# Attention, gated layer and leaky layer on one core: where the last 20 weight blocks of layer 2 are converted

## The chip, the cores and the metric

The kernel runs on one core of a Trainium2 chip. The metric is the device time of one execution, in microseconds (us); of several runs the median counts. TensorE (PE; PEld is its weight load) multiplies, VectorE (DVE), ScalarE (ACT) and GpSimd (POOL) work on tiles, SyncE (SP) issues the DMA transfers. Every engine takes its instructions in the order of the program.

## The reference

Three layers in a row, in float32. An attention whose keys and queries are hashed into buckets (2 batches, 8 heads, 768 positions, 64 columns), then a gated layer (1536 tokens, 512 to 1536 to 512), then a layer with a leaky activation (512 to 2048 to 512). What matters here are the two layers behind the attention:

```python
g = x @ w_gate                                  # layer 1
silu = g * (1.0 / (1.0 + np.exp(-g)))
x = silu * (x @ w_val) @ w_out
h = x @ w_in                                    # layer 2
g = np.maximum(h, 0.0) + alpha * np.minimum(h, 0.0)
out = g @ w_out
```

The weights reach the chip as 64-bit numbers (two 32-bit words each) and have to be converted to float32 there.

## The kernel before

The 1536 tokens are three chunks of 512 (`W`). Layer 1 runs in three stages, `stage1(0)`, `stage1(1)` and `stage1(2)`; the first two are interleaved with the attention, the third runs alone. Layer 2 runs in three passes, `stage2(1)`, `stage2(2)`, `stage2(0)`. "The third stage" is `stage1(2)`, "pass 1" is `stage2(1)`; pass 1 reads chunk 1, which the second stage of layer 1 left, and not what the third stage computes.

**Weights as two parts.** TensorE gets a float32 weight as a high part (rounded on ScalarE, L580, "h") and a low part (the rest, L587, "l": alternately on GpSimd and VectorE), and an activation likewise (`xh`, `xl`; `gh` by L635 on ScalarE, `gl` by L638 on GpSimd). A block of 128 x 512 weights costs 12 matmuls, three (`mm3`, L643 to L645, or `mm_out`, L648 to L650) for each of four slices. The low part is read by the third matmul of a slice in `mm3` and by the second in `mm_out`.

**The third stage.** It loops over f = 0 to 11 (`F1`). Each f multiplies two blocks of 12 matmuls (gate, value); ScalarE, VectorE and GpSimd then form `gh` and `gl` (L620, L623, L626, L635, L638). After f = 4 and f = 8 and at the end, `quad` multiplies four output blocks of 12 matmuls. So it has 24 + 12 blocks. Their high and low parts were stored in DRAM in the first stage; SyncE loads them back (L535, `wb<-w`, 512 KB each) into four buffers. A load waits until TensorE is through with the block four places earlier.

**Layer 2 and its blocks.** A pass loops over f = 0 to 18. At f < 16 it multiplies block hp of f (12 matmuls, into `hp`) and VectorE makes the activation (L629 `leak`, L632 `leak_sum`), ScalarE `gh`, GpSimd `gl`. At f >= 3 (`D2`) it multiplies block op of f - 3 (12 matmuls into `op`). TensorE's order is hp0, hp1, hp2, hp3, op0, hp4, op1, hp5, op2 and so on. All 32 blocks of layer 2 stay in one tile `w` (`fin.w`) as float32. The first 12 in order of use ("early") are converted during the first two stages, written to DRAM (`whole`) and read back (L531). The other 20 ("late", op4 to op15 and hp8 to hp15) are converted straight into the tile.

**Converting a block.** SyncE loads the raw block (L523, 512 KB) into one of two buffers (`RAWB`). Then `round64` runs one operation on ScalarE (L540, the low word), two on VectorE (L541, L543, the high word) and one on GpSimd (L545, the sum). `w_late` is a generator: each step converts the block loaded two steps before and loads the next, so 22 steps do 20 blocks. The next raw load into a buffer waits for L540, L541 and L543 of the block that was there.

The scheduler of the language orders the instructions of an engine; those handed to `pin` (raw loads, L540, L541, L545, loads of early blocks) keep the order of the program among themselves.

Of the kernel before, what the change touches and what calls it, by code (L numbers as in the profile page):

```python
# [22 lines left out]
RAWB = 2  # L23
# [25 lines left out]
def lsh_attention_moe_kernel(  # L49
# [23 lines left out]
    F1 = DFF // P  # L73
# [392 lines left out]
    def quad_at(f):  # L466

        return f // QF - 1 if f % QF == 0 and f else None
# [23 lines left out]
    late = [w for w in o2 if w not in early]  # L492
# [22 lines left out]
    def raw_load(w):  # L515
        t = wp.tile([P, 512, 2], I32, tag="raw64", name="raw64", bufs=RAWB)
        if F1O <= w < F2I:
            q, e = divmod(w - F1O, KD)
            src = wblk[F1O + q * QF:F1O + (q + 1) * QF, :, e * P:(e + 1) * P].bitcast(I32)
            pin(nc.sync.dma_start(out=t.rearrange("p (f c) t -> p f (c t)", f=QF),  # L520
                                  in_=src.rearrange("f p c -> p f c")))
        else:
            pin(nc.sync.dma_start(out=t, in_=wblk[w].bitcast(I32).rearrange("p (f t) -> p f t", t=2)))  # L523
        return t
# [12 lines left out]
    def round64(t, a):  # L537

        r = wp.tile([P, 512], I32, tag="wr", name="wr", bufs=2)
        pin(nc.scalar.activation(out=r, in_=t.bitcast(U32)[:, :, 0], func=AF.Copy, scale=float(2.0 ** -29)))  # L540
        pin(nc.vector.tensor_scalar(out=a, in0=t[:, :, 1], scalar1=3, scalar2=0x3FFFFFF8,  # L541
                                    op0=ALU.logical_shift_left, op1=ALU.bitwise_and))
        nc.vector.scalar_tensor_tensor(out=a, in0=t[:, :, 1], scalar=-0x40000000, in1=a,  # L543
                                       op0=ALU.bitwise_and, op1=ALU.bitwise_or)
        pin(nc.gpsimd.tensor_tensor(out=a, in0=a, in1=r, op=ALU.add))  # L545
# [10 lines left out]
    def w_late():  # L556

        rs = []
        for w in late + [None] * RAWB:
            if len(rs) == RAWB or w is None:  # L560
                r, v = rs.pop(0)
                round64(r, fin.w[:, v - F2I, :].bitcast(I32))
            if w is not None:
                rs.append((raw_load(w), w))
            yield
# [45 lines left out]
    def w_next():  # L611
        i = ws.used
        w_ahead(i)
        ws.used += 1
        t = ready.pop(i)
        return [t[:, k, :].rearrange("p (k e) -> p k e", e=P) for k in range(2)]


    def gate_tanh(gp, ex):
        nc.scalar.activation(out=ex, in_=gp, func=AF.Tanh, scale=0.5)  # L620

    def gate_mul(gp, ex):
        nc.vector.scalar_tensor_tensor(out=ex, in0=ex, scalar=1.0, in1=gp, op0=ALU.add, op1=ALU.mult)  # L623

    def gate_val(vp, ex):
        nc.vector.scalar_tensor_tensor(out=ex, in0=ex, scalar=0.5, in1=vp, op0=ALU.mult, op1=ALU.mult)  # L626

    def leak(hp, f, ex):
        nc.vector.tensor_scalar(out=ex, in0=hp, scalar1=0.0, scalar2=al[:, f:f + 1], op0=ALU.min, op1=ALU.mult)  # L629

    def leak_sum(hp, ex):
        nc.vector.scalar_tensor_tensor(out=ex, in0=hp, scalar=0.0, in1=ex, op0=ALU.max, op1=ALU.add)  # L632

    def split_h(h, ex):
        nc.scalar.activation(out=h, in_=ex, func=AF.Copy)  # L635

    def split_l(h, l, ex):
        nc.gpsimd.tensor_tensor(out=l, in0=ex, in1=f32(h), op=ALU.subtract)  # L638

    def mm3(pt, w, ah, al_, first, last):  # L640

        h, l = w
        nc.tensor.matmul(pt, lhsT=h, rhs=ah, start=first, stop=False)  # L643
        nc.tensor.matmul(pt, lhsT=h, rhs=al_, start=False, stop=False)  # L644
        nc.tensor.matmul(pt, lhsT=l, rhs=ah, start=False, stop=last)  # L645
# [16 lines left out]
    def gate_bank():  # L662
        tag = at.tag["gates"][at.gates % len(at.tag["gates"])]
        at.gates += 1
        return at.ps.tile([P, W], F32, tag=tag, name="gp", bufs=at.nb[tag])

    def quad(q, acc, gs, xh, xl):

        for e in range(KD):
            h, l = flat(w_next())  # L670
            yp = gate_bank()
            for i in range(QF):
                sl = slice(i * P, (i + 1) * P)
                mm3(yp, (h[:, sl], l[:, sl]), *gs[q * QF + i], i == 0, i == QF - 1)
                if i == 1:
                    yield
            if q == 0:
                nc.scalar.activation(out=acc[:, e, :], in_=yp, func=AF.Copy)
            else:
                nc.vector.tensor_tensor(out=acc[:, e, :], in0=yp, in1=acc[:, e, :], op=ALU.add)  # L680
            if q == F1 // QF - 1:
                nc.scalar.activation(out=xh[:, e, :], in_=acc[:, e, :], func=AF.Copy)
                eng = nc.gpsimd if ws.busy else nc.vector
                eng.tensor_tensor(out=xl[:, e, :], in0=acc[:, e, :], in1=f32(xh)[:, e, :], op=ALU.subtract)
            yield

    def stage1(c, conv=()):

        xh, xl = chunk(c)
        acc = at.lt.tile([P, KD, W], F32, tag="acc", name="acc", bufs=1)  # L690
        gs = {}
        conv = iter(conv)
        for f in range(F1):
            for _ in range(-(-(len(late) + RAWB) // F1)):
                next(conv, 0)
            ps = []
            ex = tmp()
            for tag in "GY":
                pt = gate_bank()
                w = w_next()  # L700
                for kk in range(KD):
                    mm3(pt, (w[0][:, kk, :], w[1][:, kk, :]), xh[:, kk, :], xl[:, kk, :], kk == 0, kk == KD - 1)
                    if kk == 1:
                        yield
                if tag == "G":
                    gate_tanh(pt, ex)
                    gate_mul(pt, ex)
                    yield
            gs[f] = g_tiles()
            gate_val(pt, ex)  # L710
            split_h(gs[f][0], ex)
            split_l(gs[f][0], gs[f][1], ex)
            yield
            q = quad_at(f)
            if q is not None:
                yield from quad(q, acc, gs, xh, xl)
        yield from quad(F1 // QF - 1, acc, gs, xh, xl)

    def stage2(c):

        xh, xl = chunk(c)
        t0 = c * W
        ops, gs = [], {}
        for f in range(F2 + D2):
            if f < F2:
                tag = ("G", "Y", "G", "po")[f % 4]
                hp = at.ps.tile([P, W], F32, tag=tag, name="hp2", bufs=at.nb[tag])
                w = w_next()
                for kk in range(KD):
                    mm3(hp, (w[0][:, kk, :], w[1][:, kk, :]), xh[:, kk, :], xl[:, kk, :], kk == 0, kk == KD - 1)  # L730
                ex = tmp()
                gs[f] = g_tiles()
                leak(hp, f, ex)
                leak_sum(hp, ex)
                split_h(gs[f][0], ex)
                split_l(gs[f][0], gs[f][1], ex)
            if f >= D2:
                fo = f - D2
                h, l = flat(w_next())
                a, b_ = gs.pop(fo)  # L740
                if fo == 0:
                    ops = [at.ps.tile([P, 512], F32, tag=t, name="op", bufs=at.nb[t]) for t in "SSST"]
                for i in range(W // P):
                    sl = slice(i * P, (i + 1) * P)
                    mm_out(ops[i], a[:, sl], b_[:, sl], h, l, fo == 0, fo == F2 - 1)
        for i in range(W // P):
            out_rows(t0 + i * P, ops[i], i, fin.pool.tile([P, W], F32, tag="ob", name="ob", bufs=4))
# [4 lines left out]
    def tmp():  # L752
        if fin.pool:
            return fin.pool.tile([P, W], F32, tag="ex2", name="ex2", bufs=NEX[1])
        return at.lt.tile([P, W], F32, tag="ex", name="ex", bufs=NEX[0])

    def g_tiles():
        return [at.lt.tile([P, W], F32R, tag=t, name=t, bufs=NG1) for t in ("gh", "gl")]
# [10 lines left out]
    def chunk(c):  # L769

        if c not in CH:
            CH[c] = [tx.tile([P, KD, W], F32R, tag=n, name=n, bufs=2) for n in ("xh", "xl")]
        return CH[c]
# [74 lines left out]
    ws.busy = False  # L848
    at.gates = 0
    at.tag = dict(gates="GYTS")  # L850
    for _ in stage1(2, w_late()):
        pass
    for n, c in enumerate((1, 2, 0)):
        if n == 1:
            CH.pop(0)
            for i, t in enumerate(chunk(0)):
                nc.sync.dma_start(out=f32(t).rearrange("p k w -> p (k w)"), in_=spill[i])
        stage2(c)


# [50 lines left out]
```

## Time and profile before

| what | value |
|---|---|
| median of three runs | 864.99 us (863.51 to 867.81) |
| profiled execution, its own time | 866.91 us |
| its span, first to last instruction | 865.1 us |
| TensorE busy / mean granted clock | 827.0 us / 0.988 |
| VectorE, ScalarE, GpSimd busy | 524.5, 449.4, 366.7 us |
| third stage, first to last matmul start | 493.2 to 599.3 us |
| pass 1 of layer 2 begins | 599.3 us |

The rows in this document come from one profiled execution. Times are microseconds from the start of its span; the profiled execution's own time also holds what lies around the span. A row's "idle before" is the time in which its engine had nothing to run, with the operation that ended it. The granted clock is the share of TensorE's full clock; it has two levels, 1.2 and 2.4 GHz, and a number between them is a mean over the stretch.

### The profile page before, as it was taken

The page shows a single profiled execution, that of the slowest core. Times are in us where ns is not written, and L with a number is a line of the kernel's source. Part 1 is how long each engine was busy: PE and PEld are TensorE (multiplying, and loading weights), DVE is VectorE, ACT ScalarE, POOL GpSimd, SP SyncE. Part 2 cuts the span into 40 slices and gives each one's busy share as a digit, 9 for nine tenths or more (in the row PEclk, how much of TensorE's full clock was granted, in tenths as well). Part 3 has the DMA queues.
Part 4 walks back from the last instruction along what each step waited for, and adds up shares of the span by engine and source line. Part 5 has one row for each costly group of instructions (what it writes and reads, how often), then busy time and mean ns, then how long its engine had stood idle before and what let it go on. Part 6 is the DMA issues. An engine that isn't in the chain of part 4 may idle for free.

```text
span 865.1 us, 11230 instructions
## 1 busy us (share of the span) xinstructions
PE 827.0 (96%) x4022; PEld 692.2 (80%) x4022; DVE 524.5 (61%) x789; ACT 449.4 (52%) x738; POOL 366.7 (42%) x304
## 2 busy tenths in 40 slices
PE   6899899999898999999999999999999999999997
PEld 4788688877787888888888777777888888888886
DVE  6878988888887765765675373755433343334332
ACT  7887787677766655555543232314333333333331
POOL 5212437575553532323221453634544354435441
PEclk9999999999999999999999999999999999999999
DMA  9120446776655437454535777876000300010001
GB/s 238 39 73 28 168 144 219 247 255 222 202 197 183 159 117 283 159 196 170 180 128 192 237 268 279 322 273 214 1 1 0 147 1 1 0 49 1 1 0 49
DMA packets 57287, 122.03 MB, mean 141 GB/s; under 512 B 16912, under 2 KB 29200, under 8 KB 56720
## 3 DMA queue, kind: packets, MB, share of 16 engines
q1 hardware_dynamic: 56080, 118.51, 40.2%
q0 software_dynamic: 1008, 2.75, 1.4%
q8 instruction: 32, 0.52, 0.2%
q14 instruction: 23, 0.19, 0.1%
q10 hardware_dynamic: 144, 0.05, 0.0%
HBM read 94.03 MB, written 27.26 MB: 140 GB/s over the span
## 4 chain that ended last, share of the span: by engine, by line
PE 70%; DVE 11%; ACT 7%; DMA 5%; issue 3%; POOL 2%; SPq 0%; DVEq 0%; ACTq 0%; POOLq 0%
PE po L335 9%; PE gp L645 8%; PE gp L644 8%; PE gp L643 8%; PE op L649 5%; PE hp L644 5%; PE op L650 5%; PE hp L645 5%; PE op L648 5%; PE hp L643 5%; DMA raw<-in_wblk_dram 4%; PE S L286 2%; PE S L285 2%; DVE se L322 2%; ACT se L287 2%
## 5 line engine op out<-in xcount | busy, mean ns | idle before, releaser
L638 POOL TENSOR_TENSOR gl<-ex,gh 128x512 fp32r<-128x512 f32 x84 | 111.0, 1322 | 186.2 <-ACT gh L635 185.9
L335 PE MATMUL po<-se,vv 128*128 128x256 f32 x576 | 140.6, 384 | 2.9 <-ACT se L327 2.7
L643 PE MATMUL gp<-xh,wb 128*128 128x512 f32 x288 | 122.3, 425 | 3.2 <-DMA wb<-w 3.2
L335 PEld LDWEIGHTS po<-se,vv 128*128 128x128 f32 x576 | 107.8, 191 | 20.8 <-ACT se L327 5.2
L629 DVE TENSOR_SCALAR ex<-hp,al 128x512 f32<-128x512 f32 x48 | 36.1, 751 | 136.3 <-PE hp L645 136.3
L645 PE MATMUL gp<-xh,wb 128*128 128x512 f32 x288 | 113.7, 395 | 0.0
L644 PE MATMUL gp<-xl,wb 128*128 128x512 f32 x288 | 113.4, 394 | 0.2 <-POOL xl L364 0.2
L635 ACT ACTIVATE gh<-ex 128x512 fp32r<-128x512 f32 x84 | 52.9, 630 | 109.4 <-DVE ex L632 67.6
L580 ACT ACTIVATE wb<-w 128x512 fp32r<-128x512 f32 x96 | 60.5, 632 | 92.6 <-PE hp L645 78.3
L545 POOL TENSOR_TENSOR wt<-wt,wr 128x512 int32<-128x512 int32 x48 | 63.5, 1325 | 93.3 <-DVE wt L543 45.3
L327 ACT ACTIVATE se<-se 128x1536 f32<-128x1536 f32 x48 | 71.3, 1485 | 53.6 <-DVE se L322 53.5
L287 ACT ACTIVATE se<-S 128x512 f32<-128x512 f32 x144 | 80.6, 592 | 26.6 <-PE S L286 24.0
L285 PE MATMUL S<-QA,kt 128*128 128x256 f32 x288 | 82.5, 312 | 7.7 <-ACT se L287 3.0
L322 DVE SCALAR_TENSOR_TENSOR se<-se,mb 128x1536 f32<-128x1536 f32 x48 | 83.7, 1743 | 1.8 <-PE mb L317 1.7
L286 PE MATMUL S<-qb,kt 76*128 76x256 f32 x288 | 75.4, 290 | 4.7 <-ACT qb L204 4.5
L643 PE MATMUL hp<-xh,wb 128*128 128x512 f32 x192 | 74.7, 389 | 0.0
L644 PE MATMUL hp<-xl,wb 128*128 128x512 f32 x192 | 74.7, 389 | 0.0
L645 PE MATMUL hp<-xh,wb 128*128 128x512 f32 x192 | 74.7, 389 | 0.0
L648 PE MATMUL op<-wb,gh 128*128 128x512 f32 x192 | 74.7, 389 | 0.0
L649 PE MATMUL op<-wb,gh 128*128 128x512 f32 x192 | 74.7, 389 | 0.0
L650 PE MATMUL op<-wb,gl 128*128 128x512 f32 x192 | 74.7, 389 | 0.0
L587 POOL TENSOR_TENSOR wb<-w,wb 128x512 fp32r<-128x512 f32 x48 | 62.4, 1301 | 23.6 <-ACT wb L580 23.5
(98 smaller groups left out, 1677.3 us busy)
## 6 DMA issues: line engine op xcount, KB each, us to landing
wb<-w SPq DMA_DIRECT2D x72, 512.0 KB, 4.0
raw<-in_wblk_dram SPq DMA_DIRECT2D x68, 512.0 KB, 4.1
w<-wb SPq DMA_DIRECT2D x36, 512.0 KB, 2.9
qr<-in_q_dram SPq DMA_DIRECT2D x24, 256.0 KB, 3.2
nat<-in_k_dram SPq DMA_DIRECT2D x8, 384.0 KB, 3.4
vv<-in_v_dram SPq DMA_DIRECT2D x16, 192.0 KB, 5.0
whole<-wt SPq DMA_DIRECT2D x12, 256.0 KB, 2.2
w<-whole SPq DMA_DIRECT2D x12, 256.0 KB, 6.1
```

Of the source, the lines that this page charges most:

```text
L285: nc.tensor.matmul(pt[:, i, :], lhsT=ka[:, sl], rhs=qa, start=True, stop=False)
L286: nc.tensor.matmul(pt[:, i, :], lhsT=kb[:, sl], rhs=qb, start=False, stop=True)
L287: nc.scalar.activation(out=u.se[:, 2 * j:2 * j + 2, :], in_=pt, func=AF.Copy)
L322: nc.vector.scalar_tensor_tensor(out=u.se, in0=u.se, scalar=FLOOR, in1=u.mx[:, None, :].to_broadcast([P, NC, GQ]), op0=ALU.max, op1=ALU.su ...
L335: nc.tensor.matmul(it.po[:, u.x, :], lhsT=VV[it.b, it.p][:, kb, u.x * D:u.x * D + P], rhs=u.se[:, kb, :], start=kb == 0, stop=kb == NC - 1)
L638: nc.gpsimd.tensor_tensor(out=l, in0=ex, in1=f32(h), op=ALU.subtract)
L643: nc.tensor.matmul(pt, lhsT=h, rhs=ah, start=first, stop=False)
L644: nc.tensor.matmul(pt, lhsT=h, rhs=al_, start=False, stop=False)
L645: nc.tensor.matmul(pt, lhsT=l, rhs=ah, start=False, stop=last)
L648: nc.tensor.matmul(pt, lhsT=gh, rhs=h, start=first, stop=False)
L649: nc.tensor.matmul(pt, lhsT=gh, rhs=l, start=False, stop=False)
L650: nc.tensor.matmul(pt, lhsT=gl, rhs=h, start=False, stop=last)
```

## The change

Before, the third stage takes two steps of `w_late` at each f (22 steps over 12 f, rounded up), and all are done at f = 10. After, one step is taken ahead of the stage, one at each of its 12 f, and the other nine one at each f of pass 1, f = 0 to 8.

```diff
-    def stage1(c, conv=()):
+    def stage1(c, conv=iter(())):
...
-        conv = iter(conv)
         for f in range(F1):
-            for _ in range(-(-(len(late) + RAWB) // F1)):
-                next(conv, 0)
+            next(conv, 0)
...
-    def stage2(c):
+    def stage2(c, conv):
...
         for f in range(F2 + D2):
+            next(conv, 0)
             if f < F2:
...
-    for _ in stage1(2, w_late()):
+    late_steps = w_late()
+    for _ in range(RAWB - 1):
+        next(late_steps, 0)
+    for _ in stage1(2, late_steps):
         pass
...
-        stage2(c)
+        stage2(c, late_steps)
```

On SyncE, in the third stage (f = 0 to 3), where `wb<-w` are the stored blocks of layer 1 and `raw` the late blocks:

```order
 L523 DMA raw_4787<-in_wblk_dram 128x1024
-L523 DMA raw_4794<-in_wblk_dram 128x1024
 L535 DMA wb<-w_78 128x1024
 L535 DMA wb<-w_79 128x1024
-L523 DMA raw_4839<-in_wblk_dram 128x1024
-L523 DMA raw_4846<-in_wblk_dram 128x1024
+L523 DMA raw_4832<-in_wblk_dram 128x1024
 L535 DMA wb<-w_80 128x1024
-L523 DMA raw_4891<-in_wblk_dram 128x1024
-L523 DMA raw_4898<-in_wblk_dram 128x1024
 L535 DMA wb<-w_81 128x1024
+L523 DMA raw_4877<-in_wblk_dram 128x1024
```

Pairs of raw loads between the weight loads have become single ones, one for two weight loads.

On GpSimd, from the last gl of the third stage into pass 1, before. The weights' low halves (L587) are in turn those of hp0, hp2, op0, op1, op2, op3; the gl (L638) behind them are those of f = 0 to 4:

```order
-L638 TENSOR_TENSOR gl<-ex_5426,gh 128x512
-L587 TENSOR_TENSOR wb_5517<-w_4738,wb_5517 128x512
-L587 TENSOR_TENSOR wb_5541<-w_4738,wb_5541 128x512
-L587 TENSOR_TENSOR wb_5570<-w_4738,wb_5570 128x512
-L587 TENSOR_TENSOR wb_5618<-w_4738,wb_5618 128x512
-L638 TENSOR_TENSOR gl<-ex_5561,gh 128x512
-L638 TENSOR_TENSOR gl<-ex_5585,gh 128x512
-L587 TENSOR_TENSOR wb_5662<-w_4738,wb_5662 128x512
-L638 TENSOR_TENSOR gl<-ex_5609,gh 128x512
-L638 TENSOR_TENSOR gl<-ex_5633,gh 128x512
-L587 TENSOR_TENSOR wb_5701<-w_4738,wb_5701 128x512
-L638 TENSOR_TENSOR gl<-ex_5677,gh 128x512
```

The same place after the change, from the low halves of hp0 and hp2 on; the low halves are now wb_5525 for op0, wb_5587 for op1 and, two rows behind the last one shown, wb_5638 for op2:

```order
+L587 TENSOR_TENSOR wb_5458<-w_4738,wb_5458 128x512
+L587 TENSOR_TENSOR wb_5489<-w_4738,wb_5489 128x512
+L545 TENSOR_TENSOR w_4738<-w_4738,wr 128x512
+L638 TENSOR_TENSOR gl<-ex_5509,gh 128x512
+L545 TENSOR_TENSOR w_4738<-w_4738,wr 128x512
+L638 TENSOR_TENSOR gl<-ex_5540,gh 128x512
+L587 TENSOR_TENSOR wb_5525<-w_4738,wb_5525 128x512
+L545 TENSOR_TENSOR w_4738<-w_4738,wr 128x512
+L587 TENSOR_TENSOR wb_5587<-w_4738,wb_5587 128x512
+L638 TENSOR_TENSOR gl<-ex_5571,gh 128x512
+L545 TENSOR_TENSOR w_4738<-w_4738,wr 128x512
+L638 TENSOR_TENSOR gl<-ex_5602,gh 128x512
```

The low half of op0 stood ahead of every gl of the pass and now stands behind two conversions and two gl; then a conversion, gl of f = 3 and another conversion stand ahead of the low half of op2.

## Rows read from the trace of the kernel before

**Rows 1.** The page, section 1: busy us (share of the span) and instructions by engine.

```profile
PE 827.0 (96%) x4022; PEld 692.2 (80%) x4022; DVE 524.5 (61%) x789; ACT 449.4 (52%) x738; POOL 366.7 (42%) x304
```

**Rows 2.** Timeline of PE, third stage: start us, us, instruction, [idle before <-releaser].

```profile
493.19 0.39 PE L643 MATMUL gp<-xh,wb 128*128 128x512 f32 x1
...
517.44 0.39 PE L645 MATMUL gp<-xh,wb 128*128 128x512 f32 x1
520.99 0.76 PE L643 MATMUL gp<-xh,wb 128*128 128x512 f32 x1 [3.16 <-DMA wb<-w]
...
524.05 0.40 PE L644 MATMUL gp<-xl,wb 128*128 128x512 f32 x1
...
560.90 0.39 PE L645 MATMUL gp<-gh,wb 128*128 128x512 f32 x1
562.05 0.50 PE L643 MATMUL gp<-gh,wb 128*128 128x512 f32 x1 [0.77 <-DMA wb<-w]
562.39 0.40 PE L644 MATMUL gp<-gl,wb 128*128 128x512 f32 x1
...
599.33 0.39 PE L643 MATMUL hp<-xh,wb 128*128 128x512 f32 x1
```

**Rows 3.** Windows: PE, PEld, DVE, ACT, POOL busy, PEclk, DMA share, GB/s.

```profile
517.40:525.30 7.90, 4.74 (x15) 3.51 (x15) 3.93 (x6) 2.33 (x4) 4.00 (x4) 0.78 0.95 354
```

**Rows 4.** Waits of SyncE's queue, 493.2 to 599.3: us, times, longest.

```profile
SPq L523 <- DVE w L543: 30.9, 16, 3.0
```

**Rows 5.** Timeline of SyncE around the long hole.

```profile
514.11 2.35 SPq L523 DMA_DIRECT2D raw<-in_wblk_dram  x2
516.51 0.90 SPq L535 DMA_DIRECT2D wb<-w  x2
```

**Rows 6.** Timeline of DVE, conversions of the third stage.

```profile
505.03 0.42 DVE L541 TENSOR_SCALAR w<-raw 128x512 int32<-128x512 int32 x1
505.49 0.69 DVE L543 SCALAR_TENSOR_TENSOR w<-raw,w 128x512 int32<-128x512 int32 x1
...
511.77 1.54 DVE L541 TENSOR_SCALAR w<-raw 128x512 int32<-128x512 int32 x1 [0.78 <-DMA raw<-in_wblk_dram]
...
514.41 1.66 DVE L543 SCALAR_TENSOR_TENSOR w<-raw,w 128x512 int32<-128x512 int32 x1
```

**Rows 7.** Timeline of POOL beside them.

```profile
511.73 1.29 POOL L638 TENSOR_TENSOR gl<-ex,gh 128x512 fp32r<-128x512 f32 x1 [0.70 <-ACT gh L635]
514.18 1.34 POOL L545 TENSOR_TENSOR w<-w,wr 128x512 int32<-128x512 int32 x1 [1.16 <-DVE w L543]
```

**Rows 8.** Groups by line, 493.2 to 599.3: busy us, mean ns, idle before.

```profile
L545 POOL TENSOR_TENSOR w<-w,wr 128x512 int32<-128x512 int32 x20 | 26.5, 1327 | 30.2 <-DVE w L543 20.4 <-ACT wr L540 9.9
L543 DVE SCALAR_TENSOR_TENSOR w<-raw,w 128x512 int32<-128x512 int32 x20 | 20.3, 1014 | 0.7
...
L541 DVE TENSOR_SCALAR w<-raw 128x512 int32<-128x512 int32 x20 | 15.4, 770 | 6.8 <-DMA raw<-in_wblk_dram 6.6
```

**Rows 9.** Windows, a stretch of pass 1; columns as in rows 3.

```profile
619.30:660.00 40.70, 40.70 (x181) 33.73 (x180) 14.21 (x22) 13.86 (x22) 19.62 (x16) 1.00 0.00 0
```

**Rows 10.** DMA issues, 480 to 606: count, size, median us to landing.

```profile
wb<-w SPq DMA_DIRECT2D x38, 512.0 KB, 4.5
...
w<-whole SPq DMA_DIRECT2D x12, 256.0 KB, 6.1
```

**Rows 11.** Timeline of POOL in pass 1.

```profile
640.37 1.29 POOL L638 TENSOR_TENSOR gl<-ex,gh 128x512 fp32r<-128x512 f32 x1 [2.90 <-ACT gh L635]
641.62 1.28 POOL L587 TENSOR_TENSOR wb<-w,wb 128x512 fp32r<-128x512 f32 x1
```

**Rows 12.** Timeline of PE, two holes in the attention.

```profile
237.94 0.39 PE L286 MATMUL S<-qb,kt 76*128 76x256 f32 x1 [2.21 <-ACT qb L204]
...
264.05 0.39 PE L286 MATMUL S<-qb,kt 76*128 76x256 f32 x1 [2.29 <-ACT qb L204]
```

**Rows 13.** Windows around these holes; columns as in rows 3.

```profile
262.00:269.00 7.00, 4.95 (x22) 4.39 (x23) 3.45 (x6) 5.35 (x10) 2.24 (x2) 0.76 0.50 184
236.00:243.00 7.00, 5.06 (x30) 4.48 (x31) 4.50 (x8) 5.63 (x11) 4.11 (x4) 1.00 0.66 231
```

## The prediction

> **What bounds the kernel now.** I read the page first, then TensorE row by row in the third stage, then the queue that ends its holes, then the engines behind that queue. The page gives TensorE 96% of the span [rows 1]: only its holes and its slow clock can be won or lost. In the third stage of layer 1 its matmuls follow each other every 0.2267 us (107 steps from 493.19 to 517.44 [rows 2]). The stage has 432 of them (24 gate and 12 output blocks of 12), 97.9 us at that pace; it takes 599.33 - 493.19 = 106.1 us, 8.2 more [rows 2]:
> - 517.44 to 520.99: a hole for a weight block, 3.55 - 0.23 = 3.32 us. The seven steps behind it take 3.06 us in place of 1.59, at a granted clock of 0.78 over the stretch (part of it at the lower level, 1.2 GHz) [rows 3]: 1.47.
> - Three short holes for weight blocks, each with the slow step behind it. The largest is shown: from 560.90 to 562.39 two steps take 1.49 us in place of 0.45, 1.04 lost. The other two, counted alike, lose 0.52 and 0.82: 2.38 in all.
>
> Weight holes and their slow clock are 3.32 + 1.47 + 2.38 = 7.17 us. The remaining 1.0 is mostly the wait for the last gl, no weight. What is late is the issue of the transfers: SyncE stands before raw loads until VectorE's L543 has read the buffer, 30.9 us in 16 waits [rows 4], and weight loads queue behind. Ahead of the long hole it issues two raw loads from 514.11, and only from 516.51 the weight load that TensorE starts on at 520.99 [rows 5, 2]. VectorE is late because of GpSimd: L541 takes 0.42 us alone (505.03), but 1.54 from 511.77, where GpSimd works from 511.73 to 513.02; L543 takes 0.69 alone and 1.66 from 514.41, GpSimd being busy until 515.52 [rows 6, 7]. They end 0.29 and 0.55 us after GpSimd does. Over the stage their means are 770 and 1014 ns [rows 8]: these operations, with all operands in SBUF, take turns with GpSimd.
>
> In layer 2's first pass TensorE has no hole, the DMA is idle, GpSimd is busy 19.6 of 40.7 us and VectorE 14.2 [rows 9].
>
> **The change, part by part.** No operation is added or removed: of 20 raw loads and 20 conversions (each L540 on ScalarE, L541 and L543 on VectorE, L545 on GpSimd) the place changes. By the order two raw loads stand ahead of the stage, as before; 11 raw loads and 11 conversions remain in it, nine conversions (f = 0 to 8) and seven raw loads come in pass 1.
>
> *Third stage.* One raw load per f instead of two. By the order it stands between two pairs of weight loads and waits for the conversion behind L626 of its f: 0.2 + 0.69 + 0.42 + 0.69 = 2.0 us after TensorE ends that f's second block. The weight load behind it waits for TensorE's next block anyway, 12 x 0.2267 = 2.72 us after the same moment, so the raw load costs it nothing. Each weight load has three blocks, 8.2 us, to land; the median is 4.5 [rows 10]. Per f three half-megabyte transfers go in 5.44 us instead of four: 289 GB/s, under the 354 moved in the long hole's stretch [rows 3]. GpSimd has two operations per f instead of three, so conversions meet it less. I take all 7.17 us as won; were half of the short holes to stay, 6.0.
>
> *Pass 1.* H is the first hp matmul, 599.33 before; it reads chunk 1, ready long before. The order now puts conversions ahead of what feeds TensorE: the low half of op0's weight, on GpSimd before any gl of the pass until now, stands behind two conversions and the gl of f = 0 and 1. I walked the engines by hand through the order with the durations of the rows: GpSimd 1.25 from start to start [rows 11], L541 and L543 0.42 and 0.6 alone or 0.3 and 0.55 behind GpSimd, ScalarE 0.6, a load 4.5. For op0: the conversion of f = 1 ends on VectorE at H+5.9; L629 and L632 bring H+7.2, gh H+7.9; GpSimd, held by that conversion's last step, does gl from H+8.4, lets VectorE in twice, and ends the low half at H+11.7. TensorE wants it after 49 matmuls, H+11.1: 0.6 late, 0.7 with the signal. For op2: up to its low half GpSimd has 12 operations (5 conversions, 4 gl, the low halves of op0, op1, op2), 15.0 us; VectorE in turn with it has 5 conversions at 0.85 and 3 low halves at 0.55, 5.9 us. That is 20.9 us from H+2.4, when VectorE comes to its first conversion: H+23.3 without a gap, wanted after 97 matmuls at H+22.0. But GpSimd stands idle 0.7 us before gl of f = 0, and 0.9 net before gl of f = 3, whose L629 sits on VectorE behind stretched conversions until H+16.8: H+24.9. TensorE loses 3.0 us, 0.7 at op0 and 2.3 at op2. The ends are 1.3 (no gaps) and 4.5 (0.2 more at each of some eight hand-overs). Behind op2 an f needs 3 x 1.25 + 0.85 + 0.55 = 5.15 of its 5.44 us: no further hole. Early blocks' loads now stand behind raw loads on SyncE; if they take 6.1 to land as before [rows 10], the walk gives 4.2 in place of 3.0.
>
> The Trainium skill (SBUF — State Buffer, the rule on the shared port pair) says that VectorE and GpSimd hold their shared port exclusively, for the whole instruction, and the loser is blocked. The rows agree that they exclude each other, but leave VectorE 0.29 and 0.55 us of it; by the page's whole instruction (0.42 and 0.69) pass 1 would lose some 1.8 us more.
>
> *Clock.* Of two holes near 2.3 us before the third stage, 2.21 left the clock at 1.00, 2.29 brought a stretch at 0.76 [rows 12, 13], as the 3.32 did. I count a fall behind the 2.3 at op2, at the price that it had here, 1.5.
>
> *Sum.* -7.2 + 3.0 + 1.5 = -2.7 us on the profiled execution's 866.9: 864.2. That execution lies 1.9 above the median of three runs (865.0); on the median: **862.3**.
>
> **The rivals.**
> - *No fall of the clock.* The same without 1.5: -4.2, 860.8. For it the 2.21, against it the other two.
> - *Pass 1 hides it all.* If the hand-overs cost less and the gaps close, the holes shrink to tenths: -7.2 to -6, 858 to 859. For it: GpSimd is idle for half of the pass, VectorE for two thirds. Against: the stretched means in the third stage.
> - *The other side: GpSimd and VectorE become the bound of pass 1.* If an f from 3 to 8 takes not 5.15 but what they took when crowded (three GpSimd operations at 1.33 [rows 8], 0.85 + 0.55 of VectorE, 0.1 for each of six hand-overs: 6.0), each of six f loses 0.56, 3.4 in all, and the clock falls a second time: -2.7 + 3.4 + 1.5 = +2.2, 867.2. From 5.65 us per f on, the kernel is slower. Against: the 1.33 holds part of VectorE's turn already.
> - *The change does not do what it says.* If raw waits only shift, weight holes stay: 4 won, 4.5 lost, 865.5. Against: the waits now end before the next weight load may go.
>
> **How the numbers follow.** The forecast 0.40, no fall 0.22, all hidden 0.20, the engines the bound 0.10, holes stay 0.08. About 0.5%, 4.3 us, is what a measurement of this kernel can tell from no change, so faster means below 860.7: all hidden, half of "no fall", a little of the forecast (its end without gaps is -4.4): 0.20 + 0.11 + 0.03 = 0.34. Slower needs 869.3: part of the engines' case with larger hand-overs, 0.06. The rest is 0.60. The range goes from 857.8 (all hidden) to 867.2 (the engines' case); beyond its ends lies under 2 in 10. The forecast's own range is 860.6 to 863.8.
>
> **What would show it.** Right: no TensorE hole for a weight block and no slow clock between 493 and the first hp matmul, which comes some 7 us sooner; SyncE's waits for L543 there shorter and no weight load late behind them; L541 and L543 nearer to 0.42 and 0.69. In pass 1 L541, L543 and L587 on VectorE stretched to 1 to 1.8 us, and two TensorE holes ended by GpSimd's L587, at about H+11 and H+22, the second of some 2.3 us with a slow clock behind it. Wrong: op0 and op2 run through without a hole, or holes go on past op2, or weight holes stay in the third stage.

## The result, and the profile after

The changed kernel takes 859.77 us (median of 6 runs, 857.15 to 861.46), the kernel before, on the same chip, 865.25 (6 runs, 863.51 to 867.81): ratio 0.992, 95% interval 0.9898 to 0.9942. It is faster by 0.6 to 1.0%, 5.5 us on the medians.

The profiled execution took 859.71 us against 866.91. The third stage (TensorE's first gp matmul of the stage to its first hp matmul) lasts 98.85 us in place of 106.14 [rows 2]; from that hp matmul to the span's end it is 857.9 - 589.35 = 268.55 in place of 865.1 - 599.33 = 265.77; and the stage begins at 490.50 in place of 493.19. So -7.29 + 2.78 - 2.69 = -7.20. The first two terms are the change. The third isn't: ahead of the stage every engine runs the same instructions in the same order, and the kernel before, run again, began its stage at 484.68 (before_again below).

Windows of the changed kernel: the third stage, the first 26 us of pass 1, and 40 us of the pass behind them (PE, PEld, DVE, ACT, POOL busy, granted clock, DMA share, GB/s).

```profile
490.50:589.35 98.85, 98.25 (x434) 81.03 (x432) 37.52 (x58) 27.92 (x47) 35.08 (x27) 1.00 0.73 246
589.35:615.00 25.65, 23.34 (x102) 18.69 (x101) 23.56 (x28) 11.80 (x21) 18.11 (x13) 1.00 0.52 185
615.00:655.00 40.00, 40.00 (x178) 33.15 (x177) 27.11 (x32) 16.25 (x28) 29.56 (x21) 1.00 0.08 27
```

Against [rows 3] the clock is 1.00 throughout, and TensorE lacks 0.6 us of busy time in the third stage (one hole, as before, for the last gl: 0.86 us in lost steps) and 2.3 in pass 1. There VectorE, at 23.56 of 25.65 us, is now the full engine; in [rows 9] it had a third of the time. TensorE's two holes of pass 1:

```profile
600.23 0.39 PE L648 MATMUL op<-wb,gh 128*128 128x512 f32 x1
601.45 0.50 PE L649 MATMUL op<-wb,gh 128*128 128x512 f32 x1 [0.84 <-POOL wb L587]
601.79 0.40 PE L650 MATMUL op<-wb,gl 128*128 128x512 f32 x1
...
612.26 0.39 PE L648 MATMUL op<-wb,gh 128*128 128x512 f32 x1
614.12 0.50 PE L649 MATMUL op<-wb,gh 128*128 128x512 f32 x1 [1.47 <-POOL wb L587]
614.46 0.40 PE L650 MATMUL op<-wb,gl 128*128 128x512 f32 x1
```

Two steps in place of two of 0.2267 each time: 1.56 - 0.45 = 1.10 lost at op0, 2.20 - 0.45 = 1.74 at op2, 2.84 in all; both end with GpSimd's low half L587. The groups of the conversions in the third stage (busy us, mean ns, idle before), to be held against [rows 8], and the waits of SyncE's queue there, against [rows 4] (first 490.5 to 589.35, then only to 579):

```profile
L545 POOL TENSOR_TENSOR w<-w,wr 128x512 int32<-128x512 int32 x11 | 14.2, 1287 | 19.2 <-DVE w L543 10.0 <-ACT wr L540 9.2
...
L543 DVE SCALAR_TENSOR_TENSOR w<-raw,w 128x512 int32<-128x512 int32 x11 | 7.6, 693 | 0.4
...
L541 DVE TENSOR_SCALAR w<-raw 128x512 int32<-128x512 int32 x11 | 4.6, 421 | 0.0
```

```profile
SPq L523 <- DVE w L543: 27.9, 11, 13.4
...
SPq L523 <- DVE w L543: 14.5, 10, 1.5
```

No conversion meets GpSimd any more (693 and 421 ns in place of 1014 and 770). SyncE's waits before raw loads look hardly shorter, 27.9 us in place of 30.9. But one of them, 13.4 us, is that of the first raw load of pass 1: it begins in the stage's last output blocks, when all weight loads of the stage are issued, and ends at 593.48. The ten others are 14.5 us, half of before, and none holds up a weight load. The timeline of SyncE at the place of the long hole:

```profile
503.52 0.33 SPq L523 DMA_DIRECT2D raw<-in_wblk_dram  x1
504.29 3.04 SPq L535 DMA_DIRECT2D wb<-w  x2
508.96 0.33 SPq L523 DMA_DIRECT2D raw<-in_wblk_dram  x1
509.73 3.04 SPq L535 DMA_DIRECT2D wb<-w  x2
```

The raw load goes, and 0.77 us later a weight load, whose buffer came free only then; the next weight load follows 2.72 us after it, one block of TensorE. A beat of 5.44 us, nobody late.

### The profile page after: what moved, and what is told of

Its sections match the earlier page's. It is cut to its first block, busy times and chain, and to the rows that moved or that the text cites. A ratio compares the mean times of both kernels' runs of the same rounds, so it can differ in the third digit from the quotient of the medians.

```text
span 857.9 us, 11222 instructions
## 1 busy us (share of the span) xinstructions
PE 823.7 (96%) x4022; PEld 690.3 (80%) x4022; DVE 523.5 (61%) x789; ACT 447.5 (52%) x738; POOL 370.3 (43%) x304
## 4 chain that ended last, share of the span: by engine, by line
PE 77%; DVE 9%; ACT 6%; issue 3%; DMA 2%; POOL 2%; SPq 0%; ACTq 0%; DVEq 0%; POOLq 0%
PE po L335 10%; PE gp L645 10%; PE gp L644 10%; PE gp L643 10%; PE op L649 5%; PE op L650 5%; PE op L648 5%; PE hp L644 4%; PE hp L643 4%; PE hp L645 4%; PE S L286 3%; PE S L285 3%; DVE se L322 2%; PE mt L305 1%; ACT se L287 1%
## 5 line engine op out<-in xcount | busy, mean ns | idle before, releaser
L638 POOL TENSOR_TENSOR gl<-ex,gh 128x512 fp32r<-128x512 f32 x84 | 112.8, 1343 | 186.0 <-ACT gh L635 185.1
L545 POOL TENSOR_TENSOR wt<-wt,wr 128x512 int32<-128x512 int32 x48 | 63.4, 1324 | 93.0 <-DVE wt L543 51.5
L587 POOL TENSOR_TENSOR wb<-w,wb 128x512 fp32r<-128x512 f32 x48 | 65.2, 1359 | 19.3 <-ACT wb L580 19.3
```

## The experiments

All are read by one number, the length of the third stage: 24 gate and 12 output blocks at 2.72 us are 97.9, and with the hole for the last gl 98.8 is the floor. (The stage of each row is that of one execution. R: raw buffers; a time with a count is a median, one without it, but for the first row, one execution. Ratios are to runs of before on the same chip, whose medians went from 865.25 to 869.6.)

| kernel | conversions per f of stage 3 | R | raw loads issued by | stage 3, us | time, us | ratio to before, 95% |
|---|---|---|---|---|---|---|
| before | 2 | 2 | SyncE | 106.14 | 865.25 | |
| before_again | 2 | 2 | SyncE | 107.01 | 859.26 | |
| before_nosum | 2, no L545 | 2 | SyncE | 109.56 | 871.51 | |
| before_acto | 2, L540 alone | 2 | SyncE | 111.72 | 870.88 | |
| before_half | 1 per half f | 2 | SyncE | 104.91 | 863.64 (10 runs) | 0.9951 (0.9928 to 0.9974) |
| before_rawq | 2 | 2 | GpSimd | 105.86 | 866.35 (10) | 0.9983 (0.9947 to 1.002) |
| before_ring3 | 2 | 3 | SyncE | 106.31 | 866.34 (10) | 0.9976 (0.9943 to 1.001) |
| before_ring3_acto | 2, L540 alone | 3 | SyncE | 101.83 | 862.80 | |
| before_ring3_rawq | 2 | 3 | GpSimd | 98.85 | 858.73 (4) | 0.9869 (0.9842 to 0.9896) |
| after | 1 | 2 | SyncE | 98.85 | 859.77 (6) | 0.992 (0.9898 to 0.9942) |
| after_traffic | 1 | 2 | SyncE | 98.82 | 859.01 | |
| late_f3 | 1 | 2 | SyncE | 98.85 | 856.08 (5) | 0.9881 (0.9859 to 0.9903) |
| after_novec1 | 1 | 2 | SyncE | 98.82 | 855.37 | |

**The first four: GpSimd, the traffic, and pass 1.** My theory was that GpSimd holds up VectorE's part of a conversion, and with it SyncE and the weights; the rival, that four half-megabyte loads per f are too much for the DMA. *before_again* is the kernel before once more.

> The kernel before, profiled once more. If the first two stages vary from run to run, its third stage begins some us away from 493.2, and the weight holes of the third stage are again 6 to 8 us in all. If the 2.9 us that the changed kernel's third stage began sooner belong to the change, it begins at 493 again.

Its stage begins 8.5 us sooner (484.68) and has its holes all the same, the longest of 2.60 us from 509.23. *before_nosum* takes GpSimd's sums out of the late blocks (the False leaves L545 out):

```diff
-                round64(r, fin.w[:, v - F2I, :].bitcast(I32))
+                round64(r, fin.w[:, v - F2I, :].bitcast(I32), False)
```

> The kernel before without the GpSimd sum of the 20 late blocks (so their high words alone are the weights): the order on all other engines and every transfer stay. If weight loads are late because VectorE is held by GpSimd, L541 and L543 fall to near 0.42 and 0.69 us on the mean, SyncE waits under 15 us for L543 in place of 30.9, and the weight holes with their slow clock go from 7.2 to under 2 us. If the traffic of four half-megabyte transfers per f is what the DMA can't carry, 6 to 7 us of holes stay.

The holes stayed, in a stage of 109.56 us. But the run took only a part of GpSimd's hold away: L543 fell from 1014 to 741 ns on the mean, L541 stayed at 766 (770 before; the L541 at 514.10 below ran beside a gl of GpSimd, 513.77 to 515.06), and SyncE still waited 29.6 us for L543. So the sums alone don't make the holes; before_acto below goes further. (That it is slower than before isn't shown: it is one execution of 871.51 us, and 13 runs of before on the same chip took 863.2 to 871.6.) The chain into the long hole, of the kernel before and then of before_nosum (start us, us, what):

```profile
506.37 5.37 DMA raw<-in_wblk_dram
...
511.77 1.55 DVE w L541
...
513.34 0.69 DVE w L543
...
514.41 1.67 DVE w L543
516.08 0.02 SPq L523
...
516.51 4.34 DMA wb<-w
520.85 0.14 issue
520.99 0.76 PE gp L643
```

```profile
507.87 6.21 DMA raw<-in_wblk_dram
...
514.10 1.26 DVE w L541
...
515.38 0.70 DVE w L543
...
517.58 6.08 DMA wb<-w
...
523.80 0.77 PE gp L643
```

Without the sums VectorE needs 3.1 us from landing to the second raw load's release (514.07 to 517.15) in place of 4.3, but the two landings of the chain (a raw block, then the weight block) take 12.3 us in place of 9.7. A weight buffer comes free three blocks, 8.16 us, ahead of its next use. In before the load that TensorE wanted at 517.67 could go at 509.5, went 7.0 us later and took 4.34: 11.34 against 8.16, with 0.14 to the start a hole of 3.32.

*after_traffic* gives the changed kernel back the half megabyte per f that the change took out of the stage, as a store of 1024 columns of a chunk, from SBUF to DRAM, that nobody waits for:

```diff
-            ps = []
+            ps = at.extra(f)
...
+    at.extra = lambda f: nc.sync.dma_start(out=extra[f], in_=f32(other).rearrange("p k w -> p (k w)")[:, 0:1024])
```

> The changed kernel with one more half-megabyte transfer at each f of the third stage, which waits for nothing and that nothing waits for: per f four transfers again, 385 GB/s. If traffic made the weight holes before, they come back with some 5 to 7 us and the time is near 866. If the waits of the queue made them, holes stay under 2 us and the time within 2 us of the changed kernel's.

```profile
498.00:578.00 80.00, 80.00 (x355) 66.24 (x354) 27.75 (x46) 21.35 (x36) 29.27 (x22) 1.00 0.93 323
```

TensorE is busy in all of this window, at a DMA share of 0.93 against 0.95 in [rows 3]. Traffic of this kind, a store beside three loads, makes no hole; four loads at that rate come with before_ring3_rawq. So neither theory explained the holes by itself. (Its pass 1, the same as the changed kernel's, lost 0.40 us at op0 and 1.74 at op2: the hole at op0 varies.) *late_f3* lets pass 1 convert from f = 3 on:

```diff
-            next(conv, 0)
+            f >= 3 and next(conv, 0)
```

> As the changed kernel, but the nine steps of pass 1 begin at f = 3 instead of f = 0. If the two holes at op0 and op2 (1.10 and 1.74 us) come from the conversions that stand ahead of their low halves on GpSimd and VectorE, both are gone and the time is some 2.8 us below the changed kernel, near 857. If pass 1 is simply short of GpSimd and VectorE, the holes move to later blocks and the time stays near 860.

Both holes of pass 1 are gone, the clock stays, and nothing comes back later (265.8 us from the first hp matmul to the end, as before): the first 40 us of its pass 1.

```profile
590.20:630.00 39.80, 39.80 (x177) 32.99 (x176) 32.29 (x40) 18.41 (x31) 28.21 (x21) 1.00 0.29 97
```

With the raw loads later, more of the early blocks' loads go out in the third stage (nine of 12 in place of four), so this run doesn't tell the conversions from the loads behind them; in the changed kernel it is GpSimd's low half that ends both holes.

**The next four: which part of the path is slow.** *before_rawq* lets GpSimd issue the late blocks' raw loads, so that weights stand behind nothing.

```diff
-                rs.append((raw_load(w), w))
+                rs.append((raw_load(w, nc.gpsimd), w))
```

> The kernel before, with the raw loads of the late blocks issued by GpSimd (right behind the sum of the conversion that frees the buffer) in place of SyncE; two conversions per f as before. Theory Q (the weights are late only because they stand in SyncE's queue behind raw loads that wait): the weight loads go out as soon as TensorE frees their buffers, the weight holes of the third stage and the slow clock behind the long one go, some 7 us, and the time is 858 to 860. Theory R (the ring of two raw buffers is too slow for two blocks per f: issue to landing 5.4 us and conversion 2.3 us make a turn of 7.7 us, where an f without a quad lasts 5.4 us): the conversions still come late, VectorE and ScalarE stand in front of the gate's instructions for them, and TensorE waits for those instead; at least 3 of the 7 us stay, the time is 862 or more.

Theory R (the ring is the two raw buffers used in turn) held. No hole of the stage is put down to a weight load any more, and the stage is as long as before: the chain into its long hole, from one raw load to the next.

```profile
505.38 6.51 DMA raw<-in_wblk_dram
...
511.98 0.68 ACT wr L540
512.65 0.49 ACT ex L620
...
513.23 1.23 POOL w L545
514.46 6.62 DMA raw<-in_wblk_dram
...
521.17 0.68 ACT wr L540
...
522.43 0.70 DVE ex L623
...
523.17 0.80 PE gp L643
```

A buffer's turn here is 514.46 - 505.38 = 9.1 us, and it should be 5.44. VectorE, ScalarE and GpSimd stand before the conversion, the gate's L623 stands behind it, and TensorE waits 3.31 us for that.

*before_half* puts one of the two steps ahead of G and one ahead of Y; in the order that came out, two raw loads still stood together at places (508.47).

> The kernel before, with its two steps per f set half an f apart (one ahead of G, one ahead of Y), so that raw loads and weight loads alternate in SyncE's queue. Theory R (the ring's turn of 7.7 us is longer than an f without a quad, 5.4 us): the rate asked of the ring is the same, so the holes stay, 5 us or more of the 8 in the third stage, and the time is within 0.4% of before. If only the clump of two raw loads at the start of an f makes the weights late: holes below 3 us, time 860 or less.

The holes became shorter (the longest 1.88, no fall of the clock behind it), the stage lost 6.1 us over the floor in place of 7.3: nearer to R, though 0.5% faster than before is a little more than R allowed. *before_acto* keeps of each conversion ScalarE's L540 alone.

> The kernel before, with each conversion of a late block cut down to ScalarE's one instruction, written straight into the weight; VectorE's two and GpSimd's sum are left out, the loads stay the same. Theory R: the ring's turn falls from 7.7 to about 6 us (landing 5.4, conversion 0.7), so the weight holes of the third stage fall from 7 us to 2 or less. If the traffic of four half-megabyte loads per f is itself too much for the weights to land in time: the holes stay, 5 us or more.

R's bound failed here: with VectorE and GpSimd out of the conversion altogether, the stage is the longest of all, 111.72. So the holes don't hang on VectorE, held by GpSimd or not, alone. The chain shows raw loads back to back (500.15 to 505.83 and 506.54 to 512.36), then a weight load issued at 513.44 that took 6.65 us. The landings took longer (medians in the stage 5.0 us for raw loads and 4.9 for weights in place of 4.1 and 4.6), and a buffer's turn, 506.54 - 500.15 = 6.39 us, is still above the 5.44 of an f, and SyncE still stood 25.3 us before raw loads: the ring stayed too slow. That the landings grew because the raw loads went sooner is my reading and not shown. *after_novec1* takes VectorE's two instructions out of the nine conversions of pass 1.

> The changed kernel, in which the nine blocks that are converted in pass 1 of layer 2 have no VectorE part (GpSimd's sum is kept, from ScalarE's half twice). If the two holes of pass 1 come from GpSimd's sums standing ahead of the low halves in its queue: they stay at about 1.1 and 1.7 us. If they come from the sum having to wait for VectorE's two instructions, which hold it and the low halves up behind it: both vanish or fall below 0.4 us, and the span is about 2.8 us shorter than that of the changed kernel.

Both holes went. GpSimd's sums are still there, though shorter (1.04 us, one operand) and in a somewhat other order (op0's low half behind one gl in place of two), so this doesn't split the holes between VectorE's part and the order.

**The last three: two limits at once.** *before_ring3* adds a raw buffer, from one of the six weight buffers of layer 2.

```diff
-WB = (3, 4, 6)
+WB = (3, 4, 5)
-        t = wp.tile([P, 512, 2], I32, tag="raw64", name="raw64", bufs=RAWB)
+        t = (fin.pool if n == 2 else wp).tile([P, 512, 2], I32, tag="raw64", name="raw64", bufs=1 if n == 2 else RAWB)
```

> The kernel before, two conversions per f as before, with a third buffer for the raw loads of the late blocks (its room taken from one of the six weight buffers of layer 2), so that a buffer has one and a half f, 8.2 us where an f has no quad, for its turn of some 7.7 us in place of one f, 5.4 us. If the ring's turn (landing and conversion) against the time that the buffers give it is what makes SyncE, and with it the weights, late: the weight holes of the third stage fall from 7 us to 2 or less, the clock does not fall there, and the time is 858 to 862 (less is possible to lose in layer 2 with five weight buffers in place of six). If the transfer engines simply can't carry four half-megabyte loads in 5.4 us: the third buffer only makes the raw loads land later, and 5 us or more of holes stay, with the share of the DMA engines above 0.9 ahead of them.

A miss for both sides: the holes stay (106.31), but no conversion waits for a landing any more, and the share of the DMA engines is 0.82 in the 8 us from 517 on, ahead of the first hole's end, not above 0.9. The chain into this hole is VectorE's until the weight load is issued:

```profile
510.86 0.69 DVE w L543
511.55 1.45 DVE w L541
...
514.61 0.68 DVE ex L623
...
516.45 0.69 DVE w L543
517.14 1.45 DVE w L541
...
518.62 1.67 DVE w L543
520.29 0.02 SPq L523
...
520.72 4.63 DMA wb<-w
...
525.39 0.50 PE gp L643
```

L543 of one f stands 516.45 - 510.86 = 5.59 us behind that of the f before: two conversions, one of them stretched by GpSimd, and L623 and L626 fill VectorE for 5.6 us, where an f without an output quad has 5.44. The weight loads wait behind raw loads that wait for it. So VectorE, as GpSimd stretches it (L541 takes 1.45 us here and L543 1.67, alone 0.42 and 0.69), is the limit in this run, where the landing isn't. *before_ring3_rawq* joins the two edits that had each done nothing.

> The kernel before, two conversions per f, with both the third raw buffer and the raw loads issued by GpSimd. Each alone left 7 to 8 us of holes in the third stage: with the third buffer alone the weights still stood behind raw loads that waited for VectorE; with GpSimd's queue alone the weights were in time and the gate waited for VectorE, which waited for raw loads. Theory J (several limits lie close together, each of them able to make the stage late alone): with both gone what is left is VectorE's own work, 5.6 us for an f where an f without a quad takes TensorE 5.4, a slip of some 0.2 us per f that the f with a quad gives back; holes of 2 us or less by the third stage's end (the 0.9 us ahead of the last low half apart), time 858 to 862. Theory T (the transfers themselves can't keep up): 5 us or more stay, as waits for weights or for raw loads, and the time is 864 or more.

```profile
492.36:591.21 98.85, 98.25 (x433) 81.01 (x432) 54.69 (x75) 33.17 (x56) 58.54 (x57) 1.00 0.88 314
497.00:530.00 33.00, 33.00 (x148) 27.31 (x147) 19.21 (x27) 11.29 (x19) 20.18 (x20) 1.00 0.95 354
...
497.00:509.00 12.00, 12.00 (x55) 9.93 (x54) 7.57 (x10) 4.14 (x7) 7.52 (x8) 1.00 0.99 379
```

Two conversions per f, all in the third stage, and no hole but the last gl's; 858.73 us. Theory J held, T fell: at 354 GB/s, what the long hole's stretch moved in [rows 3], TensorE doesn't miss a step. Nor is it quicker transfers that do it: at the median of the stage the raw loads land in 5.6 us in place of before's 4.1, the weights in 4.8 in place of 4.6. The Trainium skill (DMA: Bandwidth & Descriptors, Specifications) gives some 358 GB/s as one core's limit to and from HBM; this run differs, the 12 us from 497 on moved 379. *before_ring3_acto* is the other experiment.

> The kernel before, two conversions per f, with the third raw buffer, and each conversion of a late block cut to ScalarE's one instruction (VectorE's two and GpSimd's sum left out); raw loads on SyncE. Neither the ring nor VectorE can be late here, only the transfers and SyncE's order. Theory J: a raw load waits for nothing for long, so weights leave when their buffers come free; holes of 2 us or less. Theory T: the weights land late although they leave in time; 5 us or more of holes, landings of 6 us and more ahead of them.

Its stage lasts 101.83 us, with holes of 3.0 us above the floor, between J's 2 and T's 5: the raw loads on SyncE still wait (17.3 us in 12 waits) for ScalarE's L540, which stands behind the gate's instructions, and hold up the weights behind them.

## Why the prediction was right, and where not

- **Third stage, -7.17: right, -7.29.** All weight holes and the slow clock went, and what was to hide the raw load did hide it: it stands between two pairs of weight loads, and the weight load behind it goes only 0.77 us later, when its buffer comes free.
- **"VectorE is late because of GpSimd": the step that failed.** It rested on stretched rows that are real [rows 6, 7], and on the belief that what stretches an engine on the chain is what the chain waits for. before_nosum took GpSimd's sums away and before_acto VectorE's part as well, and the holes stayed. The runs put in its place a path with several limits of nearly the same length, in a loop: raw load, landing (4 to 6.5 us), conversion, next raw load into the same buffer, with the weight loads behind it in SyncE's order. With two buffers the loop takes 7.7 us (estimated: 5.4 for the landing, 2.3 for the conversion) to 9.1 (before_rawq) for each f of 5.44. Free the weights of it, and the gate waits (before_rawq); widen it, and VectorE's 5.59 us per f is too long (before_ring3); shorten the conversion, and the turn is still 6.39 us, with longer landings (before_acto). The edits of before_rawq and before_ring3 together are enough. So GpSimd's hold is one of several limits and not the cause. Halving the rate relieves all of them at once: that the term came out in full, though the cause named for it was only a part, was luck.
- **"SyncE's waits for L543 shorter": right**, 14.5 us in ten waits against 30.9 in 16. The eleventh, 13.4 us, cost the stage nothing: a wait of a queue costs only what stands behind it and could have gone.
- **Pass 1, +3.0: right, +2.84**, by the mechanism foretold. TensorE went on at H+12.1 and H+24.8 (H = 589.35), where the walk had the low halves ready at H+11.7 and H+24.9. By hole it was 1.10 and 1.74, foretold 0.7 and 2.3: the wait at op0 was larger, and pushed back the moment at which op2 is wanted. No later hole, as foretold. The closeness of 2.84 to 3.0 owes something to chance, as op0 lost 0.40 in after_traffic. late_f3 shows that the steps of `w_late` at f = 0 to 2 are the cause.
- **Clock, +1.5: mis-sized, 0.** The hole at op2 was 1.74, not 2.3, and the clock stayed at 1.00. That is the rival "no fall of the clock", 860.8, which is the nearest to the 859.8 measured. The forecast itself missed: 859.8 lies below its own range (860.6 to 863.8), and below 860.7 it is "faster", to which the prediction gave 0.34. The rule behind the term, a border between waits of 2.21 and 2.29 us, rested on two rows of the attention; the same trace has a fall behind a wait of 1.70 (last section).
- **The rest.** The stretches that the change touches account for -4.5 us. The interval of the ratio is -5.0 to -8.8; late_f3, whose trace gives -7.3, measured -8.4 to -12.2 us. Some of it may be that before's holes are longer in other executions: its third stage had 106.1 and 107.0 us in two, and its times spread over 863 to 874 in one series of 19, where late_f3 spread over 4. What the timed executions lost where wasn't recorded; this stays open, as does why the same first two stages end anywhere from 484.7 to 494.8 us.

## What to carry to other kernels

When a late transfer ends a stall, follow the chain round the whole loop, and compare the length of each engine's and each buffer's turn with the beat of the consumer; where several are near it, removing one can show nothing, and only removing two together (or less work per beat) does. Loads that wait for a consumer should not stand in one queue ahead of loads that are on the critical path. When work is moved into a stage with idle engines, look first at its start, where every operand is still to be made: here the same nine steps cost 2.8 us from f = 0 on, and nothing from f = 3 on.

## What the runs showed of the hardware

The length of a hole doesn't decide alone whether TensorE's clock falls. Behind a wait of 2.06 us in before_ring3 (525.39) the granted clock stayed at 1.00; behind one of 2.03 in before_nosum (563.27) it was 0.64 over the next 4.7 us, part of it at 1.2 GHz, in matmul steps of 0.43 us from 564.64 on. The two matmuls in the timeline of TensorE, each with the window behind it:

```profile
525.39 0.50 PE L643 MATMUL gp<-gh,wb 128*128 128x512 f32 x1 [2.06 <-DMA wb<-w]
...
525.39:530.00 4.61, 4.61 (x20) 3.83 (x21) 0.00 (x0) 0.60 (x1) 0.00 (x0) 1.00 0.75 279
```

```profile
563.27 0.47 PE L643 MATMUL gp<-gh,wb 128*128 128x512 f32 x1 [2.03 <-DMA wb<-w]
...
563.27:568.00 4.73, 4.73 (x14) 3.75 (x15) 0.97 (x3) 1.32 (x2) 1.27 (x1) 0.64 0.94 317
```

In the attention of the kernel before, even a wait of 1.70 us was followed by a fall:

```profile
175.25 0.39 PE L285 MATMUL S<-QA,kt 128*128 128x256 f32 x1 [1.70 <-DVE mk L198]
...
175.25:179.25 4.00, 4.00 (x17) 3.54 (x18) 3.92 (x6) 2.96 (x6) 3.68 (x4) 0.57 1.02 316
```

So the rows of 2.21 and 2.29 us that I took for a border [rows 12] are none. In the third stage and in pass 1 the waits of 1.73 us (before_half) and less left the clock alone; what decides it is open.
